# Projecting raw tokens and applying layer-norm statistics to the products, in the first pass of a two-layer attention/MLP kernel

## The chip, the cores and the metric

The kernel runs on one core of a Trainium2 chip. The metric is the device time of one execution in microseconds (us). Engines: PE is TensorE, DVE is VectorE, ACT is ScalarE, POOL is GpSimd, SP is SyncE, which issues most transfers.

## The reference

Two layers, each an attention block and an MLP on 2048 tokens of 1024 features in bf16, both behind a layer norm without scale or shift:

```python
x = x + attention(layernorm(x), wqkv, wo)   # 32 heads; each query sees 8 keys, 2 tokens apart
x = x + gelu_mlp(layernorm(x), w1, b1, w2, b2)
# ... and both once more
```

with `layernorm(x) = (x - mean) / sqrt(var + 1e-5)` over the features. In attention, the query, key and value projections are matrix products for TensorE. The scores and the weighted values, over the window of 8 keys, are elementwise products and sums; in this kernel VectorE does them.

## The kernel before

Tokens are worked in four groups of 512, each of four tiles of 128 tokens. The first group's start, where TensorE has nothing useful to do until data has been normalized, is this:

```python
    load_x(0, 0, 2)                                   # SP queue: tiles 0 and 1
    wq_first = [wpool.tile([P, KD // 2, D], BF16, name="wt") for _ in range(2)]
    for k in range(0, KD, 2):                         # SP queue: query weights, 512 KB pieces
        load_wq_piece(wq_first[k // (KD // 2)], k)
        if k < 4:
            load_x(0, 2 + k // 2, 3 + k // 2)         # tiles 2 and 3 in between
    # ...
    warm_up(14)                                       # matmuls of a zero tile
    # ln_first():
        stats(0)                                      # VectorE bn_stats, bn_aggr; ScalarE root
        stats(1)
        xn0 = norm(0)                                 # VectorE
        xn1 = norm(1, (0, 2 * P, D))
        transpose_on_pe(xn0, xa[0][:, 0, :, :], [(0, 2, act.copy), (2, 8, act.copy)])
        # ... xn1 likewise; then stats and norm of tiles 2 and 3
```

The query products of tiles 0 and 1 come first, for seven of eight column chunks, a quarter of the contraction at a time; tiles 2 and 3 are transposed in between:

```python
        for kq in range(4 if n == 0 else 0):
            for c in range(7):
                first[c] = qkv_chunk(wq, c, xnT, first.get(c), kq * (KD // 4), (kq + 1) * (KD // 4), 0, 2)
                # ... two transposes in between; ScalarE copies the finished queries to qT
```

VectorE meanwhile normalizes the next six tiles (`ln_early`: tiles 4 to 9), which DMA transposes carry to TensorE's layout. The value weights stand in the SP queue behind the first four of those transposes:

```python
            load_x(2)
            early_tiles = ln_early((1, None), (2, qk_next))
            for _ in range(NTT):
                next(early_tiles)                     # bn_stats, norm, DMA transpose
            wv = load_qkv(2)
            for _ in early_tiles:
                pass
```

After that VectorE does the attention of the first group, chunk by chunk, up to `oT`, which TensorE needs for the output projection (`acc<-wt,oT`). Until `oT` comes, TensorE does other groups' projections.

## Time and profile before

| | before |
|---|---|
| time, median of 3 (range) | 1230.11 us (1230.05 to 1230.32) |
| span in the profile | 1228.4 us |
| TensorE busy | 1221.6 us, 99% |
| VectorE busy | 861.5 us, 70% |
| first useful matmul | 8.26 us |
| VectorE begins the first group's attention products | 26.82 us |
| eighth and last write of `oT` begins | 123.51 us |

The page divides the span into 40 slices of 30.7 us, and each digit of an engine's row is the busy share of one slice in tenths. This is VectorE's row of slices in the page of the kernel before:

```profile
DVE  7999896998898999375993759937598797011001
```

An average of 70% hides that slices 2 to 4, from 31 to 123 us, read 9. TensorE is the bound by its share of the whole span, and VectorE is nearly as full in the first tenth of it.

### The profile page before, as it was taken

What the parts mean: (1) busy time and instruction counts of PE and PEld (TensorE: products, weight loads), DVE (VectorE), ACT (ScalarE), POOL (GpSimd) and SP (SyncE); (2) the same over time, 40 slices, a digit from 0 to 9 for tenths busy, and PEclk for the clock granted to TensorE, in tenths of its full rate; (3) what the DMA queues carried; (4) which work ended last, traced back from release to release, by engine and by line L of the source; (5) the groups of instructions that cost most, each with busy time, mean ns of one, the idle gap of its engine ahead of it and who ended that gap; (6) DMA issues with size and microseconds to landing.
All of it is one profiled execution on the core that took longest, in us unless ns stands there. A gap on an engine that the chain in (4) does not pass through costs nothing.

```text
span 1228.4 us, 13955 instructions
## 1 busy us (share of the span) xinstructions
PE 1221.6 (99%) x5720; PEld 632.7 (52%) x5770; DVE 861.5 (70%) x912; ACT 315.6 (26%) x497; POOL 120.9 (10%) x219
## 2 busy tenths in 40 slices
PE   9999999999999999999999999999999999999998
PEld 7666544456444564446544465444654444444444
DVE  7999896998898999375993759937599797011001
ACT  5343253014310233202431024410244001300310
POOL 2330025010101101100001000000000002000000
PEclk9999999999999999999999999999999999999999
DMA  9965674766638645856557565576664558446441
GB/s 302 290 206 164 176 233 151 202 178 199 219 128 245 188 150 166 239 170 175 161 158 230 172 171 181 157 216 201 171 200 147 186 194 209 149 159 194 156 135 52
DMA packets 223647, 226.64 MB, mean 185 GB/s; under 512 B 71824, under 2 KB 190752, under 8 KB 221536
## 3 DMA queue, kind: packets, MB, share of 16 engines
q1 hardware_dynamic: 214704, 208.69, 56.3%
q0 software_dynamic: 8880, 17.07, 4.2%
q8 instruction: 45, 0.74, 0.2%
q14 instruction: 18, 0.15, 0.0%
HBM read 189.01 MB, written 4.19 MB: 157 GB/s over the span
## 4 chain that ended last, share of the span: by engine, by line
PE 99%; DVE 0%; issue 0%; DMA 0%
PE acc L117 99%; DMA x<-in_A_x_dram 0%; DVE stats L92 0%; PE acc L211 0%; DVE xn L92 0%; DVE x L92 0%; DVE mv L92 0%; DVE rstd L92 0%
## 5 line engine op out<-in xcount | busy, mean ns | idle before, releaser
L117 PE MATMUL acc<-xnT,wt 128*128 128x512 bf16 (+1 forms) x3392 | 720.3, 375 | 0.1
L117 PEld LDWEIGHTS <-wt 128*128 128x128 bf16 x3392 | 400.8, 120 | 317.4
L117 PE MATMUL acc<-wt,hT 128*128 128x512 bf16 (+1 forms) x1780 | 386.0, 376 | 2.1
L117 PEld LDWEIGHTS <-hT 128*128 128x128 bf16 x1820 | 178.1, 98 | 209.0
L92 DVE TENSOR_TENSOR big<-big 128x1024 bf16<-128x1024 bf16 (+2 forms) x184 | 244.8, 1359 | 2.2
L92 ACT ACTIVATE hT<-acc,b1T 128x512 bf16<-128x512 f32 x224 | 152.1, 687 | 325.9 <-PE acc L117 325.8
L92 DVE TENSOR_TENSOR big<-qT,kT 128x4096 bf16<-128x4096 bf16 x64 | 143.8, 2283 | 36.3 <-ACT kT L92 35.9
L92 DVE TENSOR_TENSOR big<-abc,vT 128x4096 bf16<-128x4096 bf16 x64 | 144.6, 2284 | 11.0 <-DMA abc<-a 7.1
L92 DVE TENSOR_TENSOR tmp<-acc,b2bc 128x512 f32<-128x512 f32 x56 | 38.6, 689 | 159.8 <-PE acc L117 156.7
L92 ACT CAST qT<-acc 128x512 bf16<-128x512 f32 (+1 forms) x72 | 38.0, 543 | 276.8 <-PE acc L117 274.6
L117 PE MATMUL acc<-wt,oT 128*128 128x512 bf16 x440 | 97.6, 379 | 0.4
L92 DVE BATCH_NORM_STATS2 stats<-x 128x6 f32<-128x512 bf16 x116 | 77.4, 681 | 6.0 <-DMA x<-in_A_x_dram 5.0
L117 PEld LDWEIGHTS <-oT 128*128 128x128 bf16 x448 | 43.8, 98 | 53.0 <-issue 0.3
L92 DVE TENSOR_TENSOR x<-acc,big 128x512 bf16<-128x512 f32 (+1 forms) x9 | 5.7, 632 | 90.0 <-PE acc L117 90.0
L92 POOL TENSOR_TENSOR rstd<-mv,eps_t 128x1 f32<-128x1 f32 x54 | 16.7, 308 | 524.2 <-DVE mv L92 524.2
L92 ACT CAST vT<-acc 128x512 bf16<-128x512 f32 x64 | 37.4, 585 | 101.9 <-PE acc L117 101.9
L92 ACT CAST kT<-acc 128x512 bf16<-128x512 f32 x64 | 37.3, 584 | 64.5 <-PE acc L117 64.5
L92 DVE TENSOR_TENSOR x<-acc,x 128x512 bf16<-128x512 f32 x64 | 42.9, 670 | 5.1 <-PE acc L117 4.7
L92 DVE TENSOR_SCALAR xn<-x,mv,rstd 128x1024 bf16<-128x1024 bf16 (+2 forms) x53 | 28.5, 540 | 20.1 <-POOL rstd L92 19.9
L92 DVE TENSOR_TENSOR x<-tmp,x 128x512 bf16<-128x512 f32 x56 | 38.6, 689 | 1.4
L92 POOL DMA_DIRECT2D big<-big x24 | 13.3, 563 | 212.5 <-DVE big L92 212.5
L92 ACT ACT_TABLE_LOAD x17 | 21.8, 1283 | 38.9 <-DVE e L92 30.5
(62 smaller groups left out, 285.4 us busy)
## 6 DMA issues: line engine op xcount, KB each, us to landing
wt<-in_B_w_dram SPq DMA_DIRECT2D x56, 1024.0 KB, 5.6
wt<-in_B_w_dram SPq DMA_DIRECT2D x64, 896.0 KB, 4.8
wt<-in_A_wqkv_dram SPq DMA_DIRECT2D x46, 1024.0 KB, 5.6
wt<-in_A_wo_dram SPq DMA_DIRECT2D x16, 1024.0 KB, 5.0
abc<-a POOLq DMA_DIRECT2D x32, 256.0 KB, 4.6
big<-big POOLq DMA_DIRECT2D x24, 256.0 KB, 3.8
x<-in_A_x_dram SPq DMA_DIRECT2D x16, 256.0 KB, 7.1
out_dram<-x SPq DMA_DIRECT2D x31, 128.0 KB, 1.8
```

Source lines behind the costliest of these rows:

```text
L92: inst = f(*args, **kwargs)
L117: return pe(nc.tensor.matmul(*args, **kwargs))
```

## The change

Layer norm is linear once mean and rstd are known: `(x - mean) * rstd @ W = rstd * (x @ W - mean * colsum(W))`. So tiles 0 and 1 can be transposed raw, as soon as they land, and multiplied by the query weights while their statistics are still being computed. A column of ones beside the tokens makes the same matmuls produce `colsum(W)`. Mean and rstd lie one per partition (token) and are needed along the free axis, so four fp32 transposes on TensorE spread them. VectorE adds the term of the mean (`abc`, the corrections) and POOL multiplies by rstd. The keys and values of these tiles still need normalized tokens: POOL computes them from the raw transposed ones (below: POOL's sums). To bring row 0 of the weights early, rows are loaded one by one and from two queues, SP and ACT. The intent is to start TensorE 1 to 2 us earlier. The core of the diff:

```diff
-    for k in range(0, KD, 2):
-        load_wq_piece(wq_first[k // (KD // 2)], k)
-        if k < 4:
-            load_x(0, 2 + k // 2, 3 + k // 2)
+    for k in (2, 3):
+        load_wq_row(k, sp)
+    load_x(0, 3, 4)
+    for k in range(5, KD):
+        load_wq_row(k, sp)
@@
+    for k in (0, 1):
+        load_wq_row(k, act)
+    load_x(0, 2, 3, act)
+    load_wq_row(4, act)
@@ ln_first
+        raw = attp.tile([P, KD, NT + 2], BF16, name="vT", bufs=2)
+        vec.memset(raw[:, :, NT:NT + 2], 1.0)
+        warm_up(6, warm_ps)
+        transpose_on_pe(x[0], raw[:, :, 0:P], acc_tile())
         stats(0)
+        root(0)
+        transpose_on_pe(x[1], raw[:, :, P:NT], acc_tile(), (0, 2, KD))
+        warm_up(3, warm_ps)
         stats(1)
-        xn0 = norm(0)
-        xn1 = norm(1, (0, 2 * P, D))
-        (three transpose_on_pe calls of xn0, xn1)
+        def spread_stats(bank):
+            for i in range(4):
+                pe(nc.tensor.transpose(bank[:, i * P:(i + 1) * P], spread_in[:, i:i + 1].to_broadcast([P, P]), identf[:]))
+            act.copy(by_token[:].rearrange("p i t -> p (i t)"), bank[:])
+            for k0 in (0, KD // 2):
+                # (ks: half of the contraction)
+                pool.tensor_tensor(out=tmp[:, ks, :], in0=raw[:, ks, 0:NT], in1=less.unsqueeze(1).to_broadcast(size), op=ALU.add)
+                for tt in range(2):
+                    pool.tensor_tensor(out=xnT[:, tt, ks, :], in0=tmp[:, ks, ts], in1=rstd..., op=ALU.mult)
@@ queries
+        def finish(c):
+            vec.scalar_tensor_tensor(out=part[:, c, :], in0=less, scalar=first[c][:, NT:NT + 1], in1=first[c][:, 0:NT],
+                                     op0=ALU.mult, op1=ALU.add)
+            pool.tensor_tensor(out=qT[:, c, 0:NT], in0=part[:, c, :], in1=rstd, op=ALU.mult)
-        for c in list(first)[2:]:
-            act.copy(qT[:, c, 0:2 * P], first[c][:, 0:2 * P])
```

Cut: buffer and argument plumbing; in `ln_early` the roots moved from two POOL operations to ScalarE and a VectorE reciprocal. Seven corrections stand in VectorE's order ahead of the statistics of tile 4, the eighth behind the normalization of tile 4.

## The prediction

> **What bounds the kernel now.** I read the page first (busy shares and the slices), then the chain of waits for the first 40 us, then the timeline of the first 25 us, and last the issues to DMA and the busy time of each engine in short stretches. The page says that TensorE is the bound almost everywhere:
>
> ```profile
> span 1228.4 us, 13955 instructions
> PE 1221.6 (99%) x5720; PEld 632.7 (52%) x5770; DVE 861.5 (70%) x912; ACT 315.6 (26%) x497; POOL 120.9 (10%) x219
> ...
> PEclk9999999999999999999999999999999999999999
> ```
>
> The reader is to see that 1221.6 of 1228.4 us are TensorE. But busy includes work that the result doesn't need: the warm-up matmuls on a zero tile. So the only time to be had without removing matmuls is what stands before the first useful matmul, and that is where the change works. The chain of waits over the first 40 us shows it:
>
> ```profile
> 0.74 2.69 DMA x<-in_A_x_dram
> ...
> 3.46 1.30 DVE stats L92 x2
> ...
> 4.99 1.16 DVE stats L92 x2
> ...
> 6.44 0.55 DVE xn L92
> ...
> 7.10 0.74 DVE xn L92 x2
> ...
> 7.89 0.51 PE acc L211 x6
> 8.40 4.01 PE acc L117 x36
> 12.41 0.45 PE acc L211 x8
> ...
> 15.05 25.14 PE acc L117 x154
> ```
>
> Load of x, statistics of two tiles, their normalization, the transposes of the last tile, and from 8.3 us on nothing but TensorE. The timeline of the same stretch gives the start of the useful stream and the durations I use below:
>
> ```profile
> 0.99 6.02 PE L117 MATMUL acc<-big 128*128 128x512 bf16 x14 [0.99 <-DVE big L92]
> ...
> 7.05 1.35 PE L211 MATMUL acc<-ident,xn 128*128 128x128 bf16 x16
> ...
> 8.26 4.15 PE L117 MATMUL acc<-xnT,wt 128*128 128x256 bf16 x36
> 9.24 1.07 SPq L92 DMA_DIRECT2D wt<-in_A_wqkv_dram  x2
> 9.34 0.21 DVE L92 BATCH_NORM_AGGREGATE mv<-stats 128x2 f32<-128x12 f32 x1
> 9.65 0.29 ACT L92 ACTIVATE std<-mv,eps_t 128x1 f32<-128x1 f32 x1 [0.17 <-DVE mv L92]
> 9.93 1.29 DVE L92 BATCH_NORM_STATS2 stats<-x 128x6 f32<-128x512 bf16 x2 [0.38 <-DMA x<-in_A_x_dram]
> ```
>
> The head also leans on the loads. The engines of the DMA are full from 2 us on (first table), and the issue of the last piece of the query weights, at 4.10 us, takes 8.5 us to land (second fence, asked for a window with that issue alone), so it lands at 12.6 us:
>
> ```profile
> 2.00:3.00 1.00, 1.00 (x4) 0.30 (x2) 0.00 (x0) 0.23 (x2) 0.00 (x0) 1.00 0.96 274
> 5.00:6.00 1.00, 1.00 (x4) 0.30 (x2) 1.00 (x2) 0.29 (x1) 0.00 (x0) 1.00 0.90 266
> 9.00:10.00 1.00, 1.00 (x12) 1.00 (x10) 0.58 (x3) 0.77 (x2) 0.00 (x0) 1.00 1.05 401
> ```
>
> ```profile
> wt<-in_A_wqkv_dram SPq DMA_DIRECT2D x1, 512.0 KB, 8.5
> ```
>
> **What the Trainium skill says.** (1) "TensorE: Matmul & The Clock Gate", Part 1 (the HAM clock gate): the array starts at half rate and is released after a busy window of about 3.4 us that runs free. The trace agrees with half rate in the warm-up: 6.02 us for 14 is 0.43 us each, against 0.115 us for a matmul half as wide later (4.15 / 36). The two are never compared by PEclk, which reads 9 throughout, so a cold stretch must be read from the pitch. (2) "GPSIMD Engine Reference", section 3.1: a two-input elementwise operation of 2048 fp32 took 4497 ns, 2.2 ns an element. The kernel before has only operations of one element on POOL, so its trace can't confirm it. (3) "SBUF — State Buffer", section "Who interferes with whom": VectorE with two SBUF inputs or in its two-port modes, and GpSimd, lock each other out for a whole instruction. The trace agrees in one direction: the mean of the one-element power on POOL is 551 ns in most places but 2.62 us at 31.4 us, where VectorE runs products of 2.28 us back to back. (4) "DMA: Bandwidth & Descriptors", section "Queues, rings and completion order": each DMA engine takes turns between the queues that have work. All early loads are on one queue before, so no run shows it yet.
>
> **The change part by part.** The trick: transpose raw x, multiply by the weights, and correct the product with mean and rstd afterwards; the mean's term needs the sum of each weight column, which a column of ones in the moving operand gives. The order of the compiled instructions says what stands where.
>
> Removed from the path: statistics of tile 1 (1.29 + 0.21), a reciprocal, normalization of two tiles (0.55 + 0.73). Raw x0 lands at 3.43 (0.74 + 2.69). The new path: 6 warm-up matmuls from 0.99 at 0.43 end at 3.55; 8 transposes of x0 at half rate, 0.107 each (half the measured pitch of 0.43/4), to 4.4; 8 of x1 once it has landed, about 4.6, to 5.5; 3 more warm-ups, 1.28, to 6.75. On ScalarE meanwhile: copy of x0 1.01 (4.6 to 5.6), root 0.29, first copy of x1 0.37 (as its 128x256 row), done at 6.3. So the warm-ups and not the copies end last, and the first useful matmul starts at 6.75 instead of 8.26: minus 1.5 us.
>
> Added on TensorE: two columns in 64 matmuls of 256, 2/256 of 0.109, together 0.06 us. Four fp32 transposes in the stream have no row here; at two to three times the 56 ns of a bf16 transpose I take 0.15 each as a guess, 0.6 us. The 64 + 16 instructions of the first pass are otherwise as many as before.
>
> Weight rows: the same 3 MB have to arrive, so the last row still lands at about 12.6 us. Behind its arrival stand 7 matmuls, 8 transposes and 8 matmuls, 0.77 + 0.45 + 0.88 = 2.1 us, so the pass cannot end before 14.7, and before it ended at 16.4 (15.05 plus 12 matmuls). The whole change cannot give more than 1.7 us. Row 0 and row 1 are now issued by ScalarE behind its table load, at 2.25 and 2.7 us. Taking turns with the SP queue at 0.67 us per 256 KB (12.6 us less earlier landings), row 1 lands near 8 us where TensorE wants it at 7.5: plus 0.3 to 0.5 us. Later rows are in time.
>
> Off the path: POOL gets about 2x1024 + 4x512 elements of correction for the keys and values, 4096 x 2.2 ns = 9.0 us, and eight of 256 elements for the queries. VectorE loses two normalizations and gains eight products from PSUM of about 0.4 us; ScalarE loses eight query copies. These matter only if something waits for them.
>
> Sum: -1.5 + 0.06 + 0.6 + 0.4 = -0.4 to -0.5 us, 1229.6 us.
>
> **The rivals.** First, the clock: the second warm-up window contains a wait for x1 and 16 transposes. If that doesn't count as busy, the array stays at half rate up to 3.4 us longer; 16 matmuls run where 31 would, some 1.7 us lost, and the time becomes about 1231. For it: the old warm-up needed 14 matmuls, until about 6.5 us. Against: the gap is short.
>
> Second, POOL and VectorE lock each other. In the compiled order ScalarE does the root of tile 3 before it copies the spread statistics out of PSUM, so POOL begins only after tile 3's statistics, near 12.7 us, exactly when VectorE wants to normalize tile 3. If POOL's 2.2 us sum gets the port first, tile 3's transposes, wanted at about 14.5, come 1 to 2 us late: about 1231. Against: the normalization is cut into halves so that it can slip between.
>
> Third, the same POOL chain would end near 22 to 23 us, and the keys need it at about 23 to 24. It just fits; with locked stretches it might cost 1 us.
>
> Fourth, VectorE falls behind: the seven corrections come before the statistics of the next group, which begin near 17 us instead of 13.3. The DMA transposes then move from 16.7 to about 20 us and with them the value weights behind them in the SP queue, which were issued at 26.4 and whose second half took 8.8 us to 35.9, for a need at about 38. The slack of 2 us may be eaten: 0 to 1.5 us lost.
>
> Fifth, the favourable way: x1 lands early, fp32 transposes are nearly free, rows arrive in step. Then most of 1.5 us stays and the time is 1228.6.
>
> **Range and chances.** All of it lies within the first 40 us; the 1190 us after them are a dense TensorE stream that the change doesn't touch. 2% would be 24.6 us, more than the whole head is long, so faster or slower by that is nearly out of the question: 0.01 each, 0.98 for within 2%. The range: best 1228.3 (ceiling of 1.7 us nearly reached), worst 1231.6 (two rivals at once). Middle 1229.6, where the sum of parts is put.
>
> **What would show it.** In the changed profile: the first matmul on vT near 6.75 us, with a pitch of 0.11 us (0.215 if cold); the fp32 transposes near 0.15 us each; a TensorE gap at row 1 of some 0.4 us; the POOL sums near 2.2 us and their start near 12.7; whether normalization of tile 3 stretches past 14.5; the first key matmul near 23 us with no idle time before it; the value matmuls without a wait for wt. I am wrong in size if the first useful matmul starts later than 7.2, if the copies of x wait for the loads, or if any TensorE gap over 1 us appears after 16 us. A change beyond 5 us would mean that something outside the head moved, which I don't see in the order of instructions.

## The result, and the profile after

| | before | after |
|---|---|---|
| time, median of 6 runs each (range) | 1230.18 (1230.05 to 1230.39) | 1233.47 (1233.33 to 1233.96) |
| span in the profile | 1228.4 | 1231.8 |
| first useful matmul | 8.26 | 7.69 |
| first pass over tiles 0 and 1 ends (the next matmul starts) | 16.21 | 17.51 |
| first key matmul | 23.19 | 24.49 |
| first attention product on VectorE | 26.82 | 32.22 |
| eighth write of `oT` begins | 123.51 | 127.69 |

The changed kernel is slower by 3.3 us: ratio 1.0027, 95% interval 1.0014 to 1.0040. A ratio is the mean time of one kernel's fast runs over that of the other's fast runs of the same rounds, so it is not quite the ratio of the medians above. The prediction, 1229.6 us with a range of 1228.3 to 1231.6, missed: the time lies above the range, and the sign is wrong. "Within 2%" was right.

The page of the changed kernel, busy us of each engine: 3.6 more on TensorE, 7.2 more on VectorE, 10.2 more on POOL.

```profile
span 1231.8 us, 14022 instructions
...
PE 1225.2 (99%) x5769; PEld 634.0 (51%) x5769; DVE 868.7 (71%) x925; ACT 314.9 (26%) x496; POOL 131.1 (11%) x223
```

The shares cannot say where 3.4 us went; the chain can. Here is the page's summary of the chain of work that ended last, shares of the span by engine, for the kernel before:

```profile
PE 99%; DVE 0%; issue 0%; DMA 0%
```

And for the changed kernel:

```profile
PE 89%; DVE 8%; DMA 1%; issue 1%; POOL 0%; ACT 0%; SPq 0%; DVEq 0%
```

The chain that ended last ran through TensorE alone before. Afterwards, roughly the first tenth of it runs through VectorE. The pieces of that chain in order of time (start, length, what) show how far:

```profile
11.85 3.36 DVE xn L92 x2
15.35 2.85 DVE abc L92 x7
...
34.42 6.70 DVE big L92 x3
...
119.57 7.88 DVE big L92 x6
127.84 2.24 PE acc L117 x9
```

The reader is to see three things: a normalization (`xn`) of two halves that takes 3.36 us, the corrections (`abc`) behind it, and then 95 us in which the chain stays mostly on VectorE until TensorE takes over at 127.84 us. TensorE's waits between 9 and 130 us, by releaser (total us, times, longest), are short; the kernel before has none there:

```profile
PE acc L117 <- DMA wt<-in_A_wqkv_dram: 1.1, 2, 0.6
PE acc L117 <- DVE oT L92: 0.2, 1, 0.2
PE acc L224 <- ACT xnT L92: 0.2, 1, 0.2
```

The one that came last is the least conspicuous: 0.2 us on `oT`, at 127.84 us. TensorE arrived at it late itself, through the head (1.30 us later at the end of the first pass) and two waits for weights (0.42 us at 39.76 and 0.64 us at 61.34). Had it arrived earlier it would have waited longer. A short wait behind late work says who came last, not how much each lost.

The converse holds too. TensorE's first matmul on `oT` starts at 126.15 us, 2.81 us later than the 123.34 of the kernel before, so a punctual `oT` alone would have won little. But the two waits for weights lead back to VectorE as well. In SP's queue these weights stand behind DMA transposes of tiles that VectorE has normalized, and are issued when those are. Before:

```profile
26.43 1.16 SPq L92 DMA_DIRECT2D wt<-in_A_wqkv_dram  x2
...
51.78 1.08 SPq L92 DMA_DIRECT2D wt<-in_A_wqkv_dram  x2
```

And after, 4.5 and 4.0 us later:

```profile
30.92 1.64 SPq L92 DMA_DIRECT2D wt<-in_A_wqkv_dram  x2
...
55.81 1.08 SPq L92 DMA_DIRECT2D wt<-in_A_wqkv_dram  x2
```

So a late VectorE reaches TensorE by two ways: through `oT` and through the weights in SP's queue. Only the 1.30 us of the head are not of that kind.

VectorE's long normalization is in its timeline (start, length, operation). Halves of tile 2 come first, then those of tile 3:

```profile
11.01 0.74 DVE L92 TENSOR_SCALAR xn<-x,mvs,rstd 128x512 bf16<-128x512 bf16 x2
...
11.85 3.58 DVE L92 TENSOR_SCALAR xn<-x,mvs,rstd 128x512 bf16<-128x512 bf16 x2
15.35 2.85 DVE L92 SCALAR_TENSOR_TENSOR abc<-tmp,acc 128x256 f32<-128x256 f32 x7
```

POOL's timeline of the same time:

```profile
11.83 2.08 POOL L92 TENSOR_TENSOR big<-vT,tmp 128x1024 f32<-128x1024 bf16 x1 [9.48 <-ACT tmp L92]
13.99 2.56 POOL L92 TENSOR_TENSOR xnT<-big,tmp 128x512 bf16<-128x512 f32 x2
```

The same instruction takes 0.41 us for tile 2 and, instruction by instruction, 2.22 and 1.44 us for tile 3. POOL started a sum 0.02 us earlier, at 11.83; VectorE's half came through when that ended, POOL's next took its turn at 13.99, and so on. Between 21 and 28 us three of the next normalizations (0.50 us before) took 1.12, 1.06 and 0.89 us.

How full VectorE is in the stretch that follows, by the table of busy time in a window (window, then its length and busy us of PE, PEld, DVE, ACT, POOL, then clock, DMA share and GB/s), before:

```profile
60.00:123.00 63.00, 63.00 (x294) 41.97 (x293) 60.65 (x51) 24.21 (x42) 10.24 (x13) 1.00 0.59 182
```

And after:

```profile
60.00:123.00 63.00, 62.36 (x290) 41.36 (x289) 61.87 (x50) 23.38 (x40) 10.26 (x13) 1.00 0.63 188
```

VectorE is busy 61.87 of 63 us after and was busy 60.65 before. There is no room in which to catch up.

### The profile page after: what moved, and what is told of

Its sections match the earlier page's. It is cut to its first block, busy times and chain, and to the rows that moved or that the text cites. A ratio compares the mean times of both kernels' runs of the same rounds, so it can differ in the third digit from the quotient of the medians.

```text
span 1231.8 us, 14022 instructions
## 1 busy us (share of the span) xinstructions
PE 1225.2 (99%) x5769; PEld 634.0 (51%) x5769; DVE 868.7 (71%) x925; ACT 314.9 (26%) x496; POOL 131.1 (11%) x223
## 4 chain that ended last, share of the span: by engine, by line
PE 89%; DVE 8%; DMA 1%; issue 1%; POOL 0%; ACT 0%; SPq 0%; DVEq 0%
PE acc L117 89%; DVE big L92 5%; DVE stats L92 1%; DVE e L92 0%; DMA x<-in_A_x_dram 0%; DVE xn L92 0%; DMA xnT<-big 0%; POOL abc L92 0%; DVE abc L92 0%; DMA abc<-big 0%; DMA abc<-a 0%; DVE tmp L92 0%; DVE oT L92 0%; DVE a L92 0%; ACT vT L92 0%
## 5 line engine op out<-in xcount | busy, mean ns | idle before, releaser
L92 ACT CAST qT<-acc 128x512 bf16<-128x512 f32 (+1 forms) x64 | 35.4, 559 | 276.7 <-PE acc L117 272.5
L92 DVE TENSOR_SCALAR xn<-x,mv,rstd 128x1024 bf16<-128x1024 bf16 x48 | 26.2, 546 | 19.9 <-POOL rstd L92 19.7
L92 POOL DMA_DIRECT2D abc<-a x32 | 17.6, 556 | 135.0 <-DVE a L92 135.0
```

What stands on the lines that cost most here:

```text
L92: inst = f(*args, **kwargs)
```

## The experiments

Theory A: VectorE bounds the first 128 us. It was late at the attention products because POOL's sums locked it out and, for a smaller part, because of the corrections; nothing between 32 and 128 us lets it catch up; TensorE's own later head vanishes in the wait. Theory B: the losses simply add: TensorE's head (1.15 us when the expectations were written; the trace gives 1.30) and the waits in the middle are each paid in full. Theory C: the slower start of the clock and the loads of two queues are the cause, in the head alone. All runs gave correct results unless it is said otherwise.

### First four: VectorE late, warm clock, no sums, loads alone

**e1_dve_late**, the kernel before with VectorE held up:

```diff
         vec.on = True
+        late = lnp.tile([P, 11, 6], F32, name="late", bufs=1)
+        for i in range(11):
+            vec.bn_stats(late[:, i, :], x[3][:, 0:HALF])
         ahead = ln_stats(tiles[0][0])
```

> The kernel before, with eleven extra statistics instructions (11 x 0.64 = 7.0 us) on VectorE just before the second group's statistics, and nothing else. Theory A (the loss of the change is VectorE's lateness alone; TensorE's later end of the first pass is absorbed by the waits that follow): the same three TensorE waits appear as in the changed kernel (value weights near 39 us, key weights near 61 us, attention output near 127 us) and the time is 1232.8 to 1233.6 us, nearly the whole loss of 3.3. Theory B (the parts add: 1.15 us from the head, 2.0 from the later waits): about 1232.2 us. Theory C (the head alone: clock and loads): 1230.2 us, no change.

Measured: 1232.47 us against 1230.20 (ratio 1.0017, interval 1.0002 to 1.0032). That is between Theory A's range and the 1232.2 of Theory B, so the time alone doesn't choose between them. First attention product 31.72 us, last `oT` 127.19. Its waits of TensorE:

```profile
PE acc L117 <- DVE oT L92: 1.9, 1, 1.9
```

Most of the loss shows as one wait for `oT`, at 127.33 us. The rest is head: in this profile the early loads landed up to 0.64 us later than in that of the kernel before, and the first key matmul came at 23.85 us instead of 23.19. What follows: lateness of VectorE, put in at 13 us, makes a loss of this kind 114 us later. The two waits for weights in the middle did not come (in the compiled order one half of the value weights now stood ahead of the transposes; the one wait for weights in this profile, 0.3 us, is at 11.96 us), and the loss came without them.

**e2_warm**, the changed kernel with nine warm-up matmuls placed so that TensorE has no gap before the first useful one:

```diff
-        warm_up(6, warm_ps)
+        warm_up(8, warm_ps)
         transpose_on_pe(x[0], raw[:, :, 0:P], acc_tile())
+        warm_up(1, warm_ps)
```

> The changed kernel with 8 instead of 6 first warm-up matmuls and one between the two sets of transposes, so that TensorE has no gap before the first useful matmul. If gaps held back the clock, full speed comes near 6.8 us as in the kernel before, and the nine matmuls at 214 ns run at 110 ns: the first pass ends 0.9 us earlier. If transposes don't count as work for the clock, it stays slow until about 9.5 us as now. For the time: theory A (VectorE sets it) 1233.2 to 1233.6 whatever the clock does; theory B and C: 1232.4 to 1232.6 if the clock comes early.

Measured: 1233.58 us (ratio 1.0026), no change. The head did improve: first useful matmul 6.91 us, its 14 matmuls took 1.75 us instead of 2.59, and the first pass ended at 16.87 instead of 17.51.

```profile
6.91 1.75 PE L117 MATMUL acc<-vT,wt 128*128 128x258 bf16 x14 [0.17 <-ACT vT L92]
```

The 0.64 us were given back in waits for weights, 1.7 us in all instead of 1.1. The last `oT` stood at 127.61. Theories B and C expect the gain to arrive; it did not.

**e3_no_sums**, the changed kernel without POOL's sums (the keys and values of two tiles come from a constant, so the result is wrong, relative error 0.61):

```diff
-            for k0 in (0, KD // 2):
-                ...                       # the six pool.tensor_tensor of the sums
+        pool.memset(xnT[:, 0:2, :, :], 1.0)
```

> The changed kernel without POOL's six corrections of the keys' and values' input (those tiles are set to one: a wrong result on purpose). Theory A with the port lock as its main cause: the normalization of tile 3 takes 0.75 us instead of 3.4, the second group's normalizations 0.55 instead of 1.1 and 0.9, VectorE is 1.5 to 2.8 us earlier at the first DMA transpose, the later waits shrink or vanish: 1231.3 to 1232. Theory B without a lock, or C: 1233.3, only the 0.2 us wait at the last transposes goes.

Measured: 1230.17 us median against 1230.20 (ratio 1.0005, 0.9988 to 1.0022; one of four runs took 1232.53), better than the expected 1231.3 to 1232. The two halves of tile 3 are back at 0.41 us each:

```profile
11.75 0.73 DVE L92 TENSOR_SCALAR xn<-x,mvs,rstd 128x512 bf16<-128x512 bf16 x2
```

First attention product 28.56 us, last `oT` 124.06: 3.66 and 3.63 us earlier than in the changed kernel. POOL is busy for a tenth of the span, but taking its sums away makes VectorE nearly punctual. That the whole loss goes needs luck besides. In this profile TensorE was at full clock by its first useful matmul, at 6.38 us, with the changed kernel's own warm-ups, and its first pass ended at 15.34 us. With the first key matmul where the changed kernel has it, TensorE alone would have ended at 1229.7 (first sum of the table below).

**e4_two_queues**, the kernel before with the changed kernel's loads (that part of the diff alone):

> The kernel before with only the loads of the changed kernel: single weight rows, some of them and the third x tile issued from ScalarE's queue. If the second queue is what makes the first two x tiles late (4.21 and 5.53 us instead of 3.43 and 4.25), the first useful matmul moves from 8.26 to about 9.4 us, and the time is 1231.0 to 1231.5. If the later landing belongs to something else, or is absorbed, 1230.2.

Measured: 1230.79 us (ratio 1.0003). The expected range was missed. Tile 1 lands at 5.40 instead of 4.25 us, as expected, but the first useful matmul was 0.65 us later (8.91), not 1.1, and 0.6 us is all the median shows. The loads by themselves cost about this; Theory C's other part, the clock, is not in this run, whose matmuls ran at full speed from the first useful one.

### Second four: how the lock and the corrections share the loss

**e5_small_sums**, the changed kernel with POOL's six sums cut into sixteen of 256 elements:

```diff
-            for k0 in (0, KD // 2):
-                ks = slice(k0, k0 + KD // 2)
-                (one add of 1024 and two multiplications of 512 elements)
+            for k0 in range(KD):
+                ks = slice(k0, k0 + 1)
+                (one add and one multiplication of 256 elements)
```

> The changed kernel with POOL's six corrections (two of 1024 and four of 512 elements) cut into sixteen of 256 elements, the same arithmetic. If VectorE waits for whole POOL instructions, each of its normalizations now waits 0.7 us at most instead of 1.3 to 2.1: tile 3 takes about 1.6 us instead of 3.4, VectorE is 1.5 to 2 us earlier at the end of the second group, the last write of the attention output comes at about 126 us instead of 127.7, and the time is 1231.5 to 1232.3. If POOL and VectorE share the port evenly instead of locking it, the cut changes nothing or costs the extra POOL instructions: 1233.4 or more.

Measured: 1231.69 us against 1230.33 (ratio 1.0011). The halves of tile 3 took 0.80 and 0.89 us, first attention product 29.98, last `oT` 125.43. The result is correct and the same arithmetic is done; the edit changes only the length of a lock, and over half of the loss is gone. (In the profiles of this run and the next the clock was early too, as in e3; e2 found no gain in that alone.)

**e6_sums_later**, the changed kernel with the sums held back until tile 3 is normalized, by a copy of one element of its result on POOL:

```diff
+            gate = lnp.tile([P, 1], BF16, name="gate", bufs=1)
+            pool.tensor_copy(gate[:], first_late[1][0][:, D - 1:D])
             for k0 in (0, KD // 2):
```

> The changed kernel with one added POOL copy of one element of the normalized tile 3, ahead of the six corrections, so that they start only when VectorE is done with tile 3. Lock theory: tile 3's normalization takes 0.75 us, the last transposes don't wait, but VectorE still waits at the second group's normalizations, which now meet more of POOL's work: net 1.0 to 2.0 us earlier, time 1231.7 to 1232.6. Without a lock: 1233.4.

Measured: 1231.55 us median (one of four runs took 1234.14; ratio 1.0015). This is just below the expected range. Tile 3's halves 0.41 us each, last `oT` 125.39. Again over half comes back. What is left comes to TensorE by the other way: it waited 1.19 us for weights, at 59.72 us, and not for `oT`.

**e7_one_queue**, the changed kernel with all early loads on the SP queue, in the order of use:

```diff
-    (rows 2, 3, tile 3, rows 5 to 7 on SP; rows 0, 1, tile 2, row 4 on ACT)
+    for k in range(KD):
+        load_wq_row(k, sp)
+        if k < 2:
+            load_x(0, 2 + k, 3 + k)
```

> The changed kernel with all early loads on the one queue of SP, in the order x0, x1, row 0, x2, row 1, x3, rows 2 to 7. The first two x tiles should land at about 3.4 and 4.25 us again (4.2 and 5.5 in the changed kernel), x3 near 8.2; the first useful matmul at about 6.7 instead of 7.7 us. VectorE has its first four statistics 0.7 to 1.0 us earlier. If VectorE sets the time, its gain goes through: 1232.4 to 1232.9; if the loss is TensorE's clock and loads, 1232.4 as well but with the gain in the first pass; if all is bound by later waits that don't move, 1233.4.

Measured: 1232.79 us (ratio 1.0019), as expected. Tile 1 lands at 4.38 us instead of 5.53 and tile 3 at 8.13 instead of 8.92. TensorE starts at 5.84 us, now waits 0.73 us for row 1, and ends the first pass 1.64 us earlier than in the changed kernel. VectorE's last `oT` came only 1.1 us earlier (126.59), and the span fell by 0.7. TensorE's gain went into waits for weights, at 39.12 and 61.14 us; it did not wait for `oT` at all:

```profile
PE acc L117 <- DMA wt<-in_A_wqkv_dram: 2.4, 2, 1.4
```

The time follows VectorE and not TensorE's head, here through the weights behind its tiles.

**e8_no_corr**, the changed kernel without sums and without corrections (wrong; ScalarE copies the queries as they are):

> The changed kernel without any correction: no POOL sums, and plain ScalarE copies in place of VectorE's eight products and POOL's eight (a wrong result on purpose). It keeps TensorE's shorter head and gives VectorE less to do than before (two normalizations gone). Theory A: VectorE is 1 to 3 us earlier than in the kernel before, the first pass ends 0.9 to 1.3 us earlier, no wait follows, and the time is 1228.9 to 1229.5, which is the most that the idea can give. If the head's gain is worth nothing even then, 1230.2.

Measured: 1230.75 us against 1230.33; expected were 1228.9 to 1229.5. A miss. The copies of the queries, put in the place of the corrections, made ScalarE late. TensorE waited 0.87 us for one of its PSUM copies at 15.96 us and ended the first pass at 16.86, so that it was now the bound, by its head. VectorE waited 2.80 us for a root from ScalarE at 18.05 us, and its first attention product, at 27.57 us, came only 1.0 us earlier than without the sums alone. The run confirms that with VectorE early TensorE's head counts, but not what the corrections cost: taking them away brought a new wait in.

### Last four: put the cures together

**e9_combined** has the edits of the last three correct kernels at once: one queue, small sums, sums later.

> The changed kernel with three cures at once: all early loads in one queue in the order of their use, the weight sums in pieces of 256 elements, and those sums held back until the fourth token tile is normalized. VectorE-lateness theory: each cure alone brought the eighth attention-output write forward by 1.1 to 2.3 us, so all three together should bring it from 127.69 to between 123.8 and 124.5 us, where the kernel before has it, and the time to 1229.8 to 1230.6 us, the level of before. Parts-add theory (1.15 us of TensorE's head plus the middle waits, each paid in full): the middle waits for weights stay at 1 to 2 us and the time at 1231.5 to 1232.5. Clock-and-loads theory (the head alone counts): first useful matmul near 5.9 us instead of 8.26, so 1228.5 to 1229.5.

Measured: 1231.64 us against 1230.37 (ratio 1.0011). Theory A's 1229.8 to 1230.6 was missed, because the cures don't add. The time lies in Theory B's range, but without the waits for weights of 1 to 2 us that Theory B expected. The last `oT` came at 125.58 us, the gain of one cure. VectorE's timeline says why:

```profile
13.43 2.86 DVE L92 SCALAR_TENSOR_TENSOR abc<-tmp,acc 128x256 f32<-128x256 f32 x7 [2.05 <-PE acc L117]
```

Unlocked, VectorE is through tile 3 at 11.4 us and then waits 2.05 us for TensorE to finish the products that the corrections need, with the statistics of tile 4 behind them in its order. What the cures gain, this wait takes. Theory A's bound itself holds: after the first pass TensorE has nothing but one wait for `oT` of 1.47 us.

**e10_act_stats** is e9 with the statistics of tiles 8 and 9 done by ScalarE, to give VectorE some 3 us:

```diff
+    def scalar_stats(t, junk):
+        act.activation(junk, x[t][:], ACT.Identity, scale=-1.0 / D, accum_out=less[:])
+        act.activation(junk, x[t][:], ACT.Square, bias=less[:], accum_out=sq[:])
+        act.activation(std[:], sq[:], ACT.Sqrt, bias=eps_t[:], scale=1.0 / D)
```

> The combined kernel, with the statistics of the third group's two token tiles computed by ScalarE instead of VectorE. VectorE-lateness theory: some 3 us of VectorE's work ahead of the attention output are gone, the eighth write comes at 121 to 122.5 us, the wait of TensorE there disappears, and the time is set by TensorE's own head and the weight waits: 1228.9 to 1230.0 us, below both kernels if the weight waits stay under 1 us. If the span does not follow the attention output, the time equals that of the combined kernel within 0.3 us.

Measured: 1235.70 us (ratio 1.0043), a clear miss: the slowest of all. ScalarE has the statistics too late, and VectorE waits 1.66 and 2.59 us for its roots. The last `oT` came at 128.45 us, and TensorE waited 4.1 us for it. Then something new appears, in the table of busy time by window (the figure behind POOL's is the mean clock):

```profile
124.00:128.00 4.00, 0.52 (x2) 0.03 (x1) 4.00 (x5) 1.26 (x3) 0.00 (x0) 0.81 0.56 186
128.00:132.00 4.00, 3.41 (x9) 1.25 (x10) 2.26 (x5) 0.00 (x0) 0.00 (x0) 0.50 0.00 0
132.00:136.00 4.00, 4.00 (x17) 1.72 (x16) 2.60 (x5) 0.00 (x0) 0.74 (x2) 0.84 0.00 0
```

After the wait the clock is at half, for matmuls of 0.43 us until 133.3 us, and that adds 2.2 us to the wait. In e1, where the wait was 1.9 us, there is nothing of the kind.

**e11_before_act_stats** is the kernel before with the same statistics on ScalarE, as a control of VectorE's slack:

> Control: the kernel before, with the same statistics computed by ScalarE. If before is bound by TensorE there (0.8 us of slack for VectorE), freeing VectorE by 3 us does not help: 1229.9 to 1230.5 us, first useful matmul at 8.3 us, eighth attention-output write anywhere from 121 to 123.5. If VectorE bounds the kernel before as well, it gains 1 us or more: below 1229.4.

Measured: 1230.87 us against 1230.37 (ratio 1.0002): the same, though a little above the expected range. But the test did not do what it was for. VectorE waited 5.57 us for ScalarE and its attention began at 28.82 us, later than 26.82, so VectorE was not freed. It shows one thing: with the last `oT` at 124.10 us instead of 123.51 the span was 1228.2, and TensorE did not wait.

**e12_stats_first** is e9 with tile 4's statistics moved ahead of the corrections, into the gap of 2.05 us, and tile 4 loaded one row earlier:

```diff
+        st["ahead"] = ln_stats(NTT, root=True)
         for c in range(7):
             finish(c)
@@
+        if k == KD - 1:
+            load_x(1, 0, 1)
         load_wq_row(k, sp)
```

> The combined kernel, with the statistics of the second group's first token tile moved on VectorE from behind the first seven corrections to ahead of them, where the combined kernel's VectorE idled 2.05 us (11.4 to 13.4 us), and that tile loaded one row of weights earlier so that it is there by then. No work is added or removed. VectorE-lateness theory: three tensor_tensor products of the first pass then start about 1.3 us earlier (30.1 to about 28.8 us), the eighth attention-output write moves from 125.58 to 124.0 to 124.6 us, and the time from 1231.64 to 1230.1 to 1230.7 us. If what is left of the loss in the combined kernel is not VectorE's lateness but something in TensorE's stream, the time stays at 1231.3 to 1231.9.

Measured: 1231.28 us against 1230.79 on this chip (ratio 1.0005, interval 0.9991 to 1.0018). By its ratio it is the nearest of all correct versions of the change to before; the absolute time missed the expected 1230.1 to 1230.7, partly because this chip ran the kernel before 0.4 us slower. The last `oT`, at 125.39 us, missed the expected 124.0 to 124.6. The gap closed and VectorE finished the last normalization 1.0 us earlier (29.1 us instead of 30.1). But the attention products moved only from 30.10 to 29.90:

```profile
29.90 6.70 DVE L92 TENSOR_TENSOR big<-qT,kT 128x4096 bf16<-128x4096 bf16 x3 [0.76 <-POOL kT L92]
```

VectorE now waits 0.76 us for POOL, whose memset of the keys' halo stands behind sums of 11.3 us (9.3 in the six pieces of the changed kernel) and multiplications of 6.3 us. The queue that VectorE waited in had moved to POOL. No version beat the kernel before.

### What the runs say together

TensorE's first key matmul (K) says how late its head is, and the last `oT` (O) how late VectorE is:

| kernel | K, us | O, us | span, us | K + 1205.2 | O + 1104.1 |
|---|---|---|---|---|---|
| before | 23.19 | 123.51 | 1228.4 | **1228.4** | 1227.6 |
| e4_two_queues | 23.82 | 124.19 | 1229.1 | **1229.0** | 1228.3 |
| e8_no_corr | 23.85 | 124.06 | 1229.2 | **1229.1** | 1228.2 |
| e11_before_act_stats | 23.16 | 124.10 | 1228.2 | **1228.4** | 1228.2 |
| e3_no_sums | 22.32 | 124.06 | 1228.2 | 1227.5 | **1228.2** |
| e6_sums_later | 22.66 | 125.39 | 1229.7 | 1227.9 | **1229.5** |
| e5_small_sums | 22.37 | 125.43 | 1229.5 | 1227.6 | **1229.5** |
| e9_combined | 22.65 | 125.58 | 1229.7 | 1227.9 | **1229.7** |
| e12_stats_first | 22.79 | 125.39 | 1229.5 | 1228.0 | **1229.5** |
| e7_one_queue | 22.85 | 126.59 | 1231.1 | 1228.1 | **1230.7** |
| e1_dve_late | 23.85 | 127.19 | 1231.0 | 1229.1 | **1231.3** |
| e2_warm | 23.85 | 127.61 | 1231.7 | 1229.1 | **1231.7** |
| after | 24.49 | 127.69 | 1231.8 | 1229.7 | **1231.8** |
| e10_act_stats | 22.82 | 128.45 | 1234.7 | 1228.0 | 1232.6 |

The two constants are read off the kernels themselves: the first off before, e4, e8 and e11, where TensorE waits for nothing after its first key matmul; the second off after, e2, e5, e9 and e12, where it waits for `oT` and the span less O is 1104.08 to 1104.11. So each row is a description and not an independent proof. The larger of the two sums gives the span within 0.4 us in every row but the last, where the half clock adds 2.2. The kernels sharing the second constant include ones whose TensorE heads differ by 2.1 us (22.37 and 24.49). In e3, e6 and e7 TensorE did not wait for `oT` but 0.43, 1.19 and 2.37 us for weights after its first key matmul. The second sum comes near there because both ways lead back to VectorE, and not because `oT` came last.

One more number says that VectorE cannot catch up: in the changed kernel and in e1, e2, e3, e5, e6, e7, e9 and e12 the last `oT` begins 95.4 to 95.6 us after the first attention product.

The 95% intervals of the ratios reach some 0.0015 (1.8 us) to either side. So the steps between single cures rest on the profiles, and not on the medians alone. The spans come from one profiled run each. The medians repeat their order, apart from neighbours within 0.5 us and from e11, whose profiled run was its fastest.

## Why the prediction was wrong

**The step that failed** is the one that made the range: "All of it lies within the first 40 us; the 1190 us after them are a dense TensorE stream that the change doesn't touch." The stream waits for VectorE: at 128 us for its attention output, and at 39.76 and 61.34 us for weights that stand in SP's queue behind its tiles. In the kernel before, VectorE is 0.8 us early at `oT` (1228.4 - 1227.6). The change made the last `oT` 4.18 us later; less 0.75 of slack this is 3.43 us, which is the difference of the spans (1231.79 - 1228.36). The slack comes from the table's constants, so this agreement is no second measurement. With the 9s in VectorE's row this could have been asked beforehand: who waits for VectorE when its full stretch ends?

**The same step capped the gain**, which the prediction named as a "ceiling" of 1.7 us. By the two sums a perfect head could only have given 0.8 us before VectorE bound the kernel, even had the change cost VectorE nothing; no run tests this. The 1.7 itself rests on a first pass that ended at 16.4 us; its last twelve matmuls start at 14.89 and not at 15.05, and end at 16.21, so that the same sum gives 1.5.

**Rival two was right in mechanism and small in size, and put in the wrong place.** POOL did take its turn 0.02 us before tile 3, at 11.83 us (expected near 12.7), and tile 3 did stretch. Its "1 to 2 us" was meant for TensorE's transposes, but TensorE came to these late itself, at 15.80 us, and waited there only 0.21 us, for a PSUM copy. What it did to VectorE, 3.58 us where 0.73 stands without sums, and three later normalizations at about twice their length, was not counted. VectorE's attention began 5.40 us later (32.22 us instead of 26.82). From the changed kernel to the one without sums (28.56) is 3.66 of these. The other 1.74 are left for the corrections and the rest: the corrections' own 3.3 us (seven in 2.85, one in 0.47), against 3.17 us of idle time (0.38 + 0.58 + 1.50 + 0.71) that VectorE's timeline shows between 9 and 27 us in the kernel before and that is gone in the changed one, and small operations, waits and later tiles around them. No run takes that remainder apart. One piece of it can be read: with the reciprocal on VectorE, and a normalization of 0.55 us instead of 0.50, each of the six tiles of `ln_early` takes VectorE about 2.04 us where no lock is in the way (e3) and 1.85 us with the old root (e1), together some 1.2 us. Of the 5.40, 1.22 us are absorbed: in the kernel before VectorE needs 96.7 us from the first product to the last `oT`, in the changed kernel 95.5. VectorE's wait for one transfer, `abc<-a`, fell from 1.90 to 0.62 us.

**Rival four had the direction**: VectorE falls behind, the transposes move (16.7 to 22.2 us, predicted 20) and the value weights come late (0.42 us of TensorE's wait at 39.76). It ended its chain there, at "0 to 1.5 us lost", where the lateness itself went on.

**The head's sum** was off too, by sign. First useful matmul: 7.69 us instead of 6.75, past the 7.2 that the prediction gave as a sign of being wrong in size. As predicted the last warm-ups end last, but they stand behind the transposes of tile 1, which landed at 5.53 instead of the 4.6 that the prediction took (and tile 0 at 4.21 instead of 3.43), with the ACT queue's loads beside them. ACT issued its first row at 0.91 us, during its table load, and not at 2.25 after it. Then nine matmuls ran at 0.214 us (rival one, about 0.95 us). The fp32 transposes were right at 0.60 us, of which 0.44 keep TensorE, a pitch of 0.11 each. The predicted wait for row 1 did not come, and an unpredicted one of 0.21 us for a PSUM copy did. So the first pass ended 1.30 us later, where a gain of 0.4 was expected:

```profile
7.69 2.59 PE L117 MATMUL acc<-vT,wt 128*128 128x258 bf16 x14
10.12 0.60 PE L273 MATMUL acc<-identf,spread_in 128*128 128x128 f32 x4
...
15.80 0.61 PE L224 MATMUL acc<-ident,xn 128*128 128x128 bf16 x8 [0.21 <-ACT xnT L92]
```

This error alone would have made 1231.5 (1230.2 + 1.30), inside the range. e2 and e7 show that it is absorbed as long as VectorE is late: both mended the head, by 0.64 and 1.64 us at the end of the first pass, and e2 gained nothing while e7's span fell by 0.7 us, less than the 1.1 that VectorE gained. With VectorE punctual it would be paid, as e8's head was. The clock's phase is not fixed either: with the same warm-ups, four of the experiments' profiles (e3, e5, e6, e8) were at full speed by their first useful matmul, at 6.4 to 7.0 us.

**Rival three** (keys late by POOL) did not come true: POOL's sums ended at 21.2 us and the keys did not wait for them.

**What stays open.** The share of the lock is measured by taking the sums away; what the corrections cost by themselves is not, since e8 put a wait for ScalarE in their place. VectorE's slack in the kernel before was read from the two sums and not tested by a run that frees VectorE; e11 was to be that and wasn't. Which of VectorE's two ways to TensorE comes last varies from run to run, `oT` in e1, e5 and e9, the weights in e6 and e7, and what decides it was not looked into. Theory A named the right engine, but of its expected times those of e1, e3, e6, e8, e9, e10 and e12 were missed, so its sizes are less sure than its direction.

## What to carry to other kernels

Before shortening the head of a kernel that is "99% TensorE", look for a second engine whose slices read 9 and find the point where TensorE next waits for it: its slack there caps any gain, and work added to it is paid from there on. Ask too which loads stand behind its results in a queue. Work given to an idle GpSimd is not free when it locks out operations of VectorE at that time (here a normalization of 0.41 us took 2.22): cut it into short pieces or order it after them, and then look for the queue that becomes the next one. And undo a loss one cause at a time but expect cures not to add, since each frees an engine only up to its next wait.

## What the Trainium skill lacked or had wrong

- "SBUF — State Buffer", section "Who interferes with whom": whoever issues first holds the shared ports for a whole instruction. The trace agrees, and adds a size: VectorE's 0.41 us took 2.22 and 1.44 us beside POOL's sums of 2.08 and 1.28 us, and 0.80 and 0.89 us beside pieces of 0.7 us, the engines taking turns. `bn_stats`, with one input, kept its 1.27 us per two halves. The section does not say that the victim's queue can carry this over 100 us.
- "GPSIMD Engine Reference", section 3.1: its 2.2 ns an element is for 2048. Here 1024 took 2.08 us (2.03 ns an element) and 256 some 0.63 to 0.81 us (2.5 to 3.2 ns), so cutting the sums in sixteen raised them from 9.3 to 11.3 us. The page has no figure for short operations of two inputs.
- "TensorE: Matmul & The Clock Gate", Part 4: it gives some 275 ns as the duration of a bf16 transpose inside a kernel (0.22 us in these traces, whose ends are modelled), but no pitch. Here they follow each other every 56 ns at full clock and 107 ns at half. It has no figure for an fp32 one of 128x128: a pitch of 110 ns here.
- The same page, Part 1: the phase of the clock varies from run to run. The runs agree: with the same warm-ups one profile was cold until 9.5 us and four were at full clock by 7.0 us. And a wait of 4.1 us brought the half clock for about 4.7 us (2.2 us lost), where one of 1.9 us did not.
- "ScalarE: Activation LUTs", section "What ACT_TABLE_LOAD costs": 1.28 us for the load itself, as measured here (1.28). It doesn't say that the engine's queue issues transfers meanwhile: the first one here was issued at 0.91 us, in a table load from 0.74 to 2.02 us.
- "DMA: Bandwidth & Descriptors", section "Queues, rings and completion order": it has the taking of turns between queues, but no figure for what that costs the first of them. Here tile 1 landed at 5.40 us instead of 4.25 when ScalarE's queue was used beside SP's (e4).
